# A gated long convolution beside an MLP: a scratch tensor laid out for 128-partition loads, and sums combined by accumulating DMAs

## The chip, the cores and the metric

The kernel runs on one core of a Trainium2 chip. The metric is the device time of one execution in microseconds, the median of several runs. One execution was also recorded by the profiler; its lines are quoted below. In them PE is TensorE (matmuls), PEld its weight loads, DVE is VectorE, ACT is ScalarE, POOL is GpSimd and SP is SyncE, which only issues DMAs here. A "q" behind an engine's name is its instruction queue.

## The reference

Everything is float32. Two branches read the same layer-normalised input, and their results are added to the input. S is 2048, D is 448, F is 1792.

```python
x  = A_q                                    # 1 x 2048 x 448
xn = layernorm(x)                           # over D, eps 1e-5
# branch A: a gated state-space convolution
k_shift = causal depthwise conv of A_k with A_shift_k (4 taps)
kv = k_shift * A_v
y  = irfft(rfft(pad(kv)) * rfft(pad(A_ssm_k)))[:S] + kv * A_ssm_D
A  = xn * y
# branch B: an MLP
h  = xn @ B_w1 + B_b1                       # 448 -> 1792
B  = mish(h) @ B_w2                         # 1792 -> 448
return x + A + B
```

## The kernel before

The 2048 positions are 8 chunks (c0 to c7) of 256 positions, each held as [128 partitions, 2, 448]. The input q and the output have the form [128, 16, 448], so one chunk is 3584 contiguous bytes per partition. The MLP walks the chunks in order. Each chunk has 7 pairs of feature blocks; a pair is worked in two *slots*: an even slot with the first-layer matmuls (`g1_mm`, L447), and an odd slot with the activation on ScalarE (`mish`, L455), its split in a high and a low half (`split`, L74 and L75) and the second-layer matmuls (`g2_mm`, L472 to L474) of the pair two earlier. There are 116 slots. When a chunk's sums are complete, `g2_evac` (L479) adds them to q; for c0 to c5 the result goes to a DRAM scratch tensor ACC, for the last two (`late`: c6, c7) to `out`.

The convolution is worked as a Fourier transform in steps that are put between the MLP's slots by a plan written out by hand: `at(slot, ...)` puts a step ahead of the slot's MLP work, `after(slot, ...)` behind it. Instructions are issued to each engine in this order, and each engine executes its own in order. The forward transforms fill slots up to about 62 and write two scratch tensors (Dh, Dkv). Then come eight octaves (slots 63 to 90): `o_load` reads a part of each (ah, av), `h2_mm`, `v2_mm` transform them (L208), `prod` multiplies them on VectorE, `i1_mm` (L251) does the first step of the inverse, and `i1_out` copies its result to the tile qe (one buffer) and writes it with one DMA from 128 partitions, on ScalarE's queue, to the scratch tensor E (L260).

The last step works on chunks again, two at a time: c6 and c7 at slot 98, c0 and c1 at 102, c2 and c3 at 106, c4 and c5 at 111 (`I2_AT`). For each chunk:

- `e_load` (L284) reads its part of E with two DMAs of 64 partitions each on POOL's queue, into one of four buffers.
- `fold` (L290, L292) forms the sum and the difference of its two halves on VectorE.
- `i2_mm` (L310) does the last transform, 16 small matmuls per chunk; two PSUM buffers.
- `gate` multiplies by the normalised input: two instructions per position row on VectorE, (q - mean) * y at L323 and times rstd plus the MLP's sums at L325. For c6 and c7 the second adds q itself, and the MLP's evacuation later adds the rest.
- `qa_load` (L299, L300) brings q and the sums from ACC for c0 to c5 on SP's queue; each has three buffers, so the loads of c3, c4 and c5 wait until the outputs of c0, c1 and c2 have gone.
- `gate_out` (L330) writes c0 to c5 to `out` on SP's queue.

The layer-norm statistics of the next chunk are small VectorE steps in a list (`drip`); `dv()` takes the next of it between other VectorE work. Their last step has a power on POOL and the normalisation that waits for it. The tiles of the last step share memory with those of the octaves, so a first use waits for the tile that lay there.

Of the kernel before, what the change touches and what calls it, by code (L numbers as in the profile page):

```python
# [7 lines left out]
F32 = mybir.dt.float32  # L8
F32R = mybir.dt.float32r
AF = mybir.ActivationFunctionType  # L10
ALU = mybir.AluOpType
# [16 lines left out]
POOL_H = {20: (0, 2)}  # L28
H0_AT = 63
OCT_AT = (65, 3)  # L30
I2_AT = {98: (6, 7), 102: (0, 1), 106: (2, 3), 111: (4, 5)}
LATE = 2
WARM = 4
WARM_N = 448
# [3 lines left out]
def tile_kernel(ctx: ExitStack, tc, q, k, v, sk, hT, sD, w1, b1, w2, c_f1, c_g, c_gi, c_i2, out):  # L38
# [15 lines left out]

    Dh = dp.tile([NO * 16, 32, D], F32, name="Dh")
    Dkv = dp.tile([NO * 16, 32, D], F32, name="Dkv")
    E = dp.tile([64, NJ * 4, D], F32, name="E")
    ACC = dp.tile([128, NJ, D], F32, name="ACC")

    f1id = cp.tile([128, 2, 128], F32, name="f1id")  # L60
    f1, ident = f1id[:, 0], f1id[:, 1]
# [21 lines left out]
    def dv(n=1):  # L83
        for _ in range(n):
            if drip:
                drip.pop(0)()
# [4 lines left out]
    def at(slot, fn, *args):  # L91
        plan.setdefault(int(slot), []).append((fn, args))
# [163 lines left out]
    def i1_out(o):  # L256
        qe = t2([128, 4, D], "qe")
        for i, p in enumerate(PS.pop(("I", o))):
            nc.scalar.copy(qe[:, 2 * i:2 * i + 2], p[:, :, :D])
        nc.scalar.dma_start(E[8 * o:8 * o + 8].rearrange("(t r) p d -> (r p) t d", t=4), qe)  # L260


    ph3 = ExitStack()
# [3 lines left out]
    def t3(shape, name, bufs=2):  # L267
        if not sp3:
            ph2.close()
            sp3.append(ph3.enter_context(tc.tile_pool(name="ph3", bufs=2, reuse_waits="tile")))  # L270
            i2 = sp3[0].tile([128, 2, 32], F32, name="i2", bufs=1)
            nc.sync.dma_start(i2, c_i2)
            sp3.append(i2)
        return sp3[0].tile(shape, F32, name=name, bufs=bufs)

    def late(c):
        return c >= NCHUNK - LATE

    def e_load(c):

        e = EE[c] = t3([128, 2, 2, D], "e3", 4)
        src = E.rearrange("(h k) (m j b) d -> j k m h b d", h=2, m=2, b=2)
        for jj in range(2):
            nc.gpsimd.dma_start(e[64 * jj:64 * jj + 64].rearrange("p h b d -> p h (b d)"),  # L284
                              src[2 * c + jj].rearrange("k m h b d -> (k m) h (b d)"))

    def fold(c):
        e = EE[c]
        x = t3([128, 2, D], "ex")
        V.tensor_add(x, e[:, 0], e[:, 1])  # L290
        dv()
        V.tensor_sub(e[:, 1], e[:, 0], e[:, 1])  # L292
        dv()
        EE[c] = x, e[:, 1]

    def qa_load(c):
        if not late(c):
            qt, ac = t3([128, 2, D], "q3", 3), t3([128, 2, D], "a3", 3)
            nc.sync.dma_start(qt, q[:, 2 * c:2 * c + 2])  # L299
            nc.sync.dma_start(ac, ACC[:, 2 * c:2 * c + 2])  # L300
            QA[c] = qt, ac

    def i2_mm(c):
        p = pc()
# [8 lines left out]

    def gate(c):
        p = PS.pop(("P", c))
        if late(c):
            x, o, e, f = Q[c], t3([128, 2, D], "z", 1), Q[c], Q[c]
        else:
            qt, ac = QA[c]
            x, o, e, f = qt, qt, ac, qt  # L320
        for jj in range(2):
            j = 2 * c + jj
            V.scalar_tensor_tensor(o[:, jj], x[:, jj], mv[:, j, 0:1], p[:, jj, :D], op0=ALU.subtract, op1=ALU.mult)  # L323
            dv()
            V.scalar_tensor_tensor(f[:, jj], o[:, jj], rstd[:, j:j + 1], e[:, jj], op0=ALU.mult, op1=ALU.add)  # L325
            dv()

    def gate_out(c):
        if not late(c):
            nc.sync.dma_start(out[:, 2 * c:2 * c + 2], QA.pop(c)[0])  # L330


    RW = {}
# [142 lines left out]
    def g2_evac(c, jjs=(0, 1)):  # L476
        x = Q[c]
        for jj in jjs:
            V.tensor_add(x[:, jj], P2.pop((c, jj))[:, :D], x[:, jj])  # L479
            dv()  # L480
            if late(c):
                nc.sync.dma_start(out[:, 2 * c + jj], x[:, jj])
        if not late(c):
            nc.sync.dma_start(ACC[:, 2 * c:2 * c + 2], x)

    def mlp_slot(s):
        i, half = divmod(s, 2)
# [81 lines left out]
    ts = sorted(I2_AT)  # L569
    for n, t in enumerate(ts):  # L570
        for m, c in enumerate(I2_AT[t]):
            at(ts[n - 2] + 1 if n > 1 else ts[0] - 4 + n, e_load, c)
            at(ts[n - 1] + (2 if m else -2 if n == 2 else -1) if n > 1 else ts[0] - 5 + m, qa_load, c)
            after(t - 3, fold, c)
            at(t, i2_mm, c)
            after(t, gate, c)
            at(t + 2 + m, gate_out, c)

    V.memset(rstd, 0.0)
    V.memset(mhalf, -0.5)  # L580
# [53 lines left out]
def _constants():  # L634
# [10 lines left out]
    f1 = np.stack([Wo.real, Wo.imag], axis=4).reshape(64, 128)  # L645
    f1 = np.concatenate([f1, f1])

    i2 = np.stack([W.real.T, W.imag.T], axis=1)[:32].reshape(4, 2, 4, 2, 64).transpose(0, 2, 1, 3, 4).reshape(64, 2, 32) / 2048
    i2 = np.concatenate([i2, i2])
    n2 = np.arange(32)[:, None] // 2 + 16 * (np.arange(32)[:, None] % 2)  # L650
    k2 = np.arange(32)[None, :]
# [2 lines left out]
    for kk in range(64):  # L654
        o, r, t = kk // 8, kk // 4 % 2, kk % 4
        g = w(n2 * (4 * kk - 1) + 256 * n2 * k2)
        G[r, 0, :, o, t, 0], G[r, 1, :, o, t, 0] = g.real, -g.imag
        G[r, 0, :, o, t, 1], G[r, 1, :, o, t, 1] = g.imag, g.real

        gt = g.T.reshape(32, 16, 2)  # L660
        GI[t, :, o, r, 0, 0], GI[t, :, o, r, 1, 0] = gt.real, gt.imag
        GI[t, :, o, r, 0, 1], GI[t, :, o, r, 1, 1] = -gt.imag, gt.real
    c = lambda a: np.ascontiguousarray(a, dtype=np.float32)
    return dict(c_f1=c(np.stack([f1, np.eye(128)], axis=1)), c_g=c(G.reshape(128, 8, 4, 2, 32)), c_gi=c(GI.reshape(128, 8, 2, 2, 64)),
                c_i2=c(i2))
# [27 lines left out]
```

## Time and profile before

| What | us |
|---|---|
| Median of 3 runs (375.63 to 376.65) | 376.12 |
| The profiled execution | 375.92 |
| Its span, first to last instruction | 373.9 |
| PE busy | 362.3 |
| DVE busy | 269.1 |
| ACT busy | 158.7 |
| POOL busy | 67.4 |

The span is what the trace shows; the time of the same execution is 2.0 us more. Busy times are shares of the whole span, and the stages differ, so what matters in a stage is read from its own windows and timelines. A row of a timeline has the start and the duration in us, the engine, the line, the operation, what it writes and reads, and the number of merged instructions; a bracket at its end gives the idle time of the engine before it and what ended that. A matmul's duration includes the pipeline, so that rows overlap.

### The profile page before, as it was taken

How to read it: one execution, taken by the hardware profiler on the slowest of the kernel's cores; microseconds unless marked ns; L12 is line 12 of the kernel's file. 1: busy time of each engine (PE TensorE's matmuls, PEld its weight loads, DVE VectorE, ACT ScalarE, POOL GpSimd, SP SyncE). 2: the span in 40 equal slices, each digit the busy share in tenths (PEclk: the TensorE clock that was granted, in tenths of full speed). 3: DMA queues.
4: the chain of work that ended last, by engine and by line, in shares of the span. 5: the costliest groups of instructions: out<-in, count | busy, mean ns of one | idle time of the engine just before them, and what ended most of it. 6: DMA issues, size and time to landing. Idle time of an engine off the chain costs nothing.

```text
span 373.9 us, 7487 instructions
## 1 busy us (share of the span) xinstructions
PE 362.3 (97%) x3128; PEld 292.6 (78%) x3128; DVE 269.1 (72%) x370; ACT 158.7 (42%) x265; POOL 67.4 (18%) x57
## 2 busy tenths in 40 slices
PE   8999999999998999999999999999999999999993
PEld 2889888888897988988886666666666799688983
DVE  4899748999959987995445745844854915799683
ACT  2785642443433324333434755553755243213220
POOL 2107002622070225320033000140000005220000
PEclk9999999999999999999999999999999999999998
DMA  8999968657695437604794687868480778999466
GB/s 308 315 319 317 396 232 246 200 162 230 163 297 181 100 66 233 196 3 121 238 296 154 214 272 248 269 236 271 160 295 22 260 285 183 221 196 284 152 199 244
DMA packets 32563, 82.11 MB, mean 220 GB/s; under 512 B 2961, under 2 KB 18194, under 8 KB 32530
## 3 DMA queue, kind: packets, MB, share of 16 engines
q1 hardware_dynamic: 22130, 51.69, 41.5%
q10 hardware_dynamic: 9120, 22.61, 20.1%
q0 software_dynamic: 1280, 7.34, 8.5%
q8 instruction: 24, 0.39, 0.4%
q14 instruction: 9, 0.07, 0.0%
HBM read 53.19 MB, written 28.44 MB: 218 GB/s over the span
## 4 chain that ended last, share of the span: by engine, by line
PE 44%; DMA 10%; DVE 9%; issue 3%; ACT 2%; POOL 1%; DVEq 0%; SPq 0%; POOLq 0%
PE pg L447 17%; PE pc L208 7%; PE pg L472 5%; PE pg L474 5%; PE pg L473 5%; DMA out_dram<-q 4%; PE pc L251 3%; DMA a<-ACC 3%; DMA e<-E 2%; PE pc L125 1%; PE pg L407 1%; DMA E<-qe 1%; DVE ex L290 1%; DVE acl L75 1%; DVE q L325 1%
## 5 line engine op out<-in xcount | busy, mean ns | idle before, releaser
L455 ACT ACTIVATE a<-pg,b1t 128x256 f32<-128x256 f32 x112 | 47.1, 473 | 119.2 <-PE pg L447 103.5
L447 PE MATMUL pg<-XH,w1h 128*128 128x256 f32 x448 | 91.1, 285 | 0.7 <-ACT XH L419 0.7
L447 PEld LDWEIGHTS pg<-XH,w1h 128*128 128x128 f32 x448 | 69.7, 188 | 17.4 <-issue 15.0
L472 PE MATMUL pg<-w2h,ach 128*128 128x448 f32 x224 | 83.1, 371 | 0.0
L473 PE MATMUL pg<-w2l,ach 128*128 128x448 f32 x224 | 81.3, 363 | 0.6 <-DVE w2l L75 0.6
L474 PE MATMUL pg<-w2h,acl 128*128 128x448 f32 x224 | 81.4, 363 | 0.0
L75 DVE TENSOR_TENSOR acl<-a,ach 128x512 fp32r<-128x512 f32 x56 | 38.7, 691 | 50.4 <-ACT ach L74 50.3
L447 PE MATMUL pg<-XL,w1h 128*128 128x256 f32 x448 | 69.6, 277 | 0.0
L447 PEld LDWEIGHTS pg<-XL,w1h 128*128 128x128 f32 x448 | 59.4, 188 | 0.1
L447 PE MATMUL pg<-XH,w1l 128*128 128x256 f32 x336 | 56.8, 278 | 0.0
L472 PEld LDWEIGHTS pg<-w2h,ach 128*128 128x128 f32 x224 | 42.0, 187 | 12.3 <-issue 9.4
L447 PEld LDWEIGHTS pg<-XH,w1l 128*128 128x128 f32 x336 | 46.8, 188 | 0.1
L473 PEld LDWEIGHTS pg<-w2l,ach 128*128 128x128 f32 x224 | 42.1, 188 | 3.5 <-DVE w2l L75 1.1
L474 PEld LDWEIGHTS pg<-w2h,acl 128*128 128x128 f32 x224 | 42.1, 188 | 2.6
L388 POOL TENSOR_TENSOR rstd<-ve,mhalf 128x2 f32<-128x2 f32 (+1 forms) x9 | 8.5, 948 | 167.6 <-DVE ve L385 162.4
L74 ACT CAST ach<-a 128x512 fp32r<-128x512 f32 x56 | 34.7, 620 | 1.8
L155 POOL TENSOR_TENSOR x<-kr,skb 128x896 f32<-128x896 f32 x8 | 17.0, 2129 | 74.8 <-DVE x L154 54.1
L172 DVE TENSOR_TENSOR x<-x 128x896 f32<-128x896 f32 x24 | 26.6, 1106 | 5.1 <-POOL x L155 4.4
L392 POOL TENSOR_SCALAR xn<-qt,mv,rstd 128x448 f32<-128x448 f32 x12 | 26.8, 2240 | 0.6
L419 ACT CAST XH<-pg 128x512 fp32r<-128x512 f32 x16 | 9.4, 588 | 37.6 <-PE pg L407 37.4
L131 ACT COPY st<-pc 128x896 f32<-128x896 f32 x16 | 14.5, 908 | 14.8 <-PE pc L125 14.8
L417 DVE TENSOR_TENSOR XL<-pg,XH 128x512 fp32r<-128x512 f32 x16 | 10.9, 687 | 13.5 <-ACT XH L419 13.3
(65 smaller groups left out, 399.9 us busy)
## 6 DMA issues: line engine op xcount, KB each, us to landing
Dh<-st ACTq DMA_DIRECT2D x16, 448.0 KB, 5.9
Dkv<-st ACTq DMA_DIRECT2D x16, 448.0 KB, 5.1
ah<-Dh SPq DMA_DIRECT2D x8, 896.0 KB, 5.4
av<-Dkv SPq DMA_DIRECT2D x8, 896.0 KB, 4.9
E<-qe ACTq DMA_DIRECT2D x8, 896.0 KB, 4.2
e<-E POOLq DMA_DIRECT2D x16, 448.0 KB, 10.3
kr<-in_k_dram SPq DMA_DIRECT2D x10, 448.0 KB, 6.3
kr<-in_w_dram SPq DMA_DIRECT2D x7, 512.0 KB, 5.8
```

The source lines that it names most:

```text
L74: nc.scalar.copy(h, raw)
L75: V.tensor_sub(l, raw, h)
L131: nc.scalar.copy(st[:, 1], o)
L155: nc.gpsimd.tensor_mul(o, KR[g - u // 2], skb[:, u:u + 1].to_broadcast([128, 2, D]))
L172: V.tensor_add(KV[g], KV[g], o)
L208: nc.tensor.matmul(p[32 * t:32 * t + 32, r, :D], g[rs, t, c], a[rs, t], start=True, stop=True, tile_position=(64 * r, 32 * t))
L392: eng.tensor_scalar(xn[:, jj, :D], Q[c][:, jj], mv[:, j, 0:1], rstd[:, j:j + 1], op0=ALU.subtract, op1=ALU.mult)
L447: nc.tensor.matmul(ps[:, n], l, r, start=n_ == 0, stop=n_ == len(mm) - 1)
L455: nc.scalar.activation(a[:, n], ps[:, n], AF.Mish, bias=b1t[:, 2 * p + n:2 * p + n + 1])
L472: nc.tensor.matmul(ps, ah[:, n, cs], w2h[:, f], start=f == 0, stop=False)
L473: nc.tensor.matmul(ps, ah[:, n, cs], w2l[:, f], start=False, stop=False)
L474: nc.tensor.matmul(ps, al[:, n, cs], w2h[:, f], start=False, stop=f == NF - 1)
```

## The change

E is laid out anew: its rows come in another order (the constants of `i1_mm` and `i2_mm` are permuted to match), so that a chunk's part is one load of 128 partitions, and the write of an octave is two DMAs of 64 partitions each. ACC is gone: `g2_evac` writes the MLP's sums of c0 to c5 to `out`, and `gate_out` adds the gated product to them by an accumulating DMA on POOL's queue. The gate of c0 to c5 has one VectorE instruction and a ScalarE multiply by rstd per row. `q_load` loads only q, with five buffers and one of the MLP's; c0 and c1 at slot 92 on SP's queue, c2 to c5 at slot 94 on POOL's. The loads of E for the first two pairs come at slots 92 and 93. The second chunk of a pair is folded and gated one slot behind the first, and the last pair is at slot 110 instead of 111, both gates directly behind it. The statistics list is emptied at slot 91.

```diff
-I2_AT = {98: (6, 7), 102: (0, 1), 106: (2, 3), 111: (4, 5)}
+I2_AT = {98: (6, 7), 102: (0, 1), 106: (2, 3), 110: (4, 5)}
...
-    E = dp.tile([64, NJ * 4, D], F32, name="E")
-    ACC = dp.tile([128, NJ, D], F32, name="ACC")
+    E = dp.tile([NJ * 4, 64, D], F32, name="E")
...
-        nc.scalar.dma_start(E[8 * o:8 * o + 8].rearrange("(t r) p d -> (r p) t d", t=4), qe)
+        for r in range(2):
+            k = 8 * (o % 4) + 4 * r
+            nc.scalar.dma_start(E.rearrange("p (k h) d -> p k h d", h=2)[:, k:k + 4, o // 4], qe[64 * r:64 * r + 64])
...
         e = EE[c] = t3([128, 2, 2, D], "e3", 4)
-        src = E.rearrange("(h k) (m j b) d -> j k m h b d", h=2, m=2, b=2)
-        for jj in range(2):
-            nc.gpsimd.dma_start(e[64 * jj:64 * jj + 64].rearrange("p h b d -> p h (b d)"),
-                              src[2 * c + jj].rearrange("k m h b d -> (k m) h (b d)"))
+        nc.gpsimd.dma_start(e.rearrange("p b h d -> p b (h d)"),
+                            E.rearrange("(b x) (k h) d -> x k b (h d)", b=2, h=2)[4 * c:4 * c + 4].rearrange("x k b d -> (x k) b d"))
...
-        V.tensor_add(x, e[:, 0], e[:, 1])
+        V.tensor_add(x, e[:, :, 0], e[:, :, 1])
         dv()
-        V.tensor_sub(e[:, 1], e[:, 0], e[:, 1])
+        V.tensor_sub(e[:, :, 1], e[:, :, 0], e[:, :, 1])
         dv()
-        EE[c] = x, e[:, 1]
-
-    def qa_load(c):
-        if not late(c):
-            qt, ac = t3([128, 2, D], "q3", 3), t3([128, 2, D], "a3", 3)
-            nc.sync.dma_start(qt, q[:, 2 * c:2 * c + 2])
-            nc.sync.dma_start(ac, ACC[:, 2 * c:2 * c + 2])
-            QA[c] = qt, ac
+        EE[c] = x, e[:, :, 1]
+
+    def q_load(c, eng=nc.sync):
+        QA[c] = mp.tile([128, 2, D], F32, name="qt", tag="qt", bufs=3) if c == 5 else t3([128, 2, D], "q3", 5)
+        eng.dma_start(QA[c], q[:, 2 * c:2 * c + 2])
...
     def gate(c):
         p = PS.pop(("P", c))
-        if late(c):
-            x, o, e, f = Q[c], t3([128, 2, D], "z", 1), Q[c], Q[c]
-        else:
-            qt, ac = QA[c]
-            x, o, e, f = qt, qt, ac, qt
         for jj in range(2):
             j = 2 * c + jj
-            V.scalar_tensor_tensor(o[:, jj], x[:, jj], mv[:, j, 0:1], p[:, jj, :D], op0=ALU.subtract, op1=ALU.mult)
+            r = rstd[:, j:j + 1]
+            x = (Q if late(c) else QA)[c][:, jj]
+            o = t3([128, D], "z") if late(c) else x
+            V.scalar_tensor_tensor(o, x, mv[:, j, 0:1], p[:, jj, :D], op0=ALU.subtract, op1=ALU.mult)
             dv()
-            V.scalar_tensor_tensor(f[:, jj], o[:, jj], rstd[:, j:j + 1], e[:, jj], op0=ALU.mult, op1=ALU.add)
-            dv()
+            if late(c):
+                V.scalar_tensor_tensor(x, o, r, x, op0=ALU.mult, op1=ALU.add)
+                dv()
+            else:
+                nc.scalar.mul(x, x, r)
 
     def gate_out(c):
         if not late(c):
-            nc.sync.dma_start(out[:, 2 * c:2 * c + 2], QA.pop(c)[0])
+            nc.gpsimd.dma_start(out[:, 2 * c:2 * c + 2], QA.pop(c), accum_op=ALU.add)
...
-            nc.sync.dma_start(ACC[:, 2 * c:2 * c + 2], x)
+            nc.sync.dma_start(out[:, 2 * c:2 * c + 2], x)
...
-            at(ts[n - 2] + 1 if n > 1 else ts[0] - 4 + n, e_load, c)
-            at(ts[n - 1] + (2 if m else -2 if n == 2 else -1) if n > 1 else ts[0] - 5 + m, qa_load, c)
-            after(t - 3, fold, c)
+            at(ts[n - 2] + 1 if n > 1 else ts[0] - 6 + n, e_load, c)
             at(t, i2_mm, c)
-            after(t, gate, c)
+            after(t if t == ts[-1] else t + m, gate, c)
             at(t + 2 + m, gate_out, c)
+            after(t - 4 + m if n else t - 3 + m, fold, c)
+    for c in range(NCHUNK - LATE):
+        at(ts[0] - (6 if c < 2 else 4), q_load, c, nc.sync if c < 2 else nc.gpsimd)
+
+    at(ts[0] - 7, lambda: dv(len(drip)))
```

More of the change, by code (lines that the diff above doesn't have):

```diff
@@ L646, in _constants @@
     f1 = np.concatenate([f1, f1])
-    i2 = np.stack([W.real.T, W.imag.T], axis=1)[:32].reshape(4, 2, 4, 2, 64).transpose(0, 2, 1, 3, 4).reshape(64, 2, 32) / 2048
+    i2 = np.stack([W.real.T, W.imag.T])[:, :32].reshape(64, 2, 32) / 2048
     i2 = np.concatenate([i2, i2])
@@ L658, in _constants @@
         G[r, 0, :, o, t, 1], G[r, 1, :, o, t, 1] = g.imag, g.real
-        gt = g.T.reshape(32, 16, 2)
-        GI[t, :, o, r, 0, 0], GI[t, :, o, r, 1, 0] = gt.real, gt.imag
-        GI[t, :, o, r, 0, 1], GI[t, :, o, r, 1, 1] = -gt.imag, gt.real
+        gt = g.T.reshape(32, 16, 2).transpose(0, 2, 1)
+        GI[t, :, o, r, 0, ..., 0], GI[t, :, o, r, 1, ..., 0] = gt.real, gt.imag
+        GI[t, :, o, r, 0, ..., 1], GI[t, :, o, r, 1, ..., 1] = -gt.imag, gt.real
     c = lambda a: np.ascontiguousarray(a, dtype=np.float32)
```

## The prediction

> **What bounds the kernel now.** I read the head of the page first, then the windows of the last stage, the timelines of TensorE and VectorE there, and last the chain of waits.
>
> ```profile
> span 373.9 us, 7487 instructions
> PE 362.3 (97%) x3128; PEld 292.6 (78%) x3128; DVE 269.1 (72%) x370; ACT 158.7 (42%) x265; POOL 67.4 (18%) x57
> PE   8999999999998999999999999999999999999993
> ```
>
> TensorE is busy 97% of the span, so only two things can shorten this kernel: holes in TensorE's row, and what lies behind its last matmul. The change touches the work from some 200 us on, its core lies behind 300. There the windows (columns: time, length, then busy time of PE, PEld, DVE, ACT, POOL, the granted clock, DMA share, GB/s) show one hole of over half a microsecond, at 320 to 324, and the end from 368 on:
>
> ```profile
> 320.00:322.00 2.00, 1.45 (x20) 0.14 (x4) 1.96 (x2) 0.00 (x0) 1.03 (x2) 1.00 1.01 219
> 322.00:324.00 2.00, 1.82 (x21) 0.99 (x20) 2.00 (x4) 0.00 (x0) 0.54 (x2) 1.00 1.02 222
> 368.00:370.00 2.00, 0.23 (x2) 0.00 (x0) 1.97 (x4) 0.00 (x0) 0.00 (x0) 1.00 0.21 84
> ```
>
> TensorE's timeline around the hole. The third column is the duration, the bracket is what ended the idle time:
>
> ```profile
> 319.62 0.57 PE L310 MATMUL pc<-ex,i 64*32 64x448 f32 x2
> ...
> 321.15 0.94 PE L310 MATMUL pc<-ex,i 64*32 64x448 f32 x4 [0.55 <-DVE ex L290]
> ...
> 323.18 0.62 PE L447 MATMUL pg<-XH,w1h 128*128 128x256 f32 x3
> ...
> 333.20 0.57 PE L310 MATMUL pc<-ex,i 64*32 64x448 f32 x2
> ...
> 334.86 0.62 PE L447 MATMUL pg<-XH,w1h 128*128 128x256 f32 x3
> ```
>
> A pair of chunks of the last transform (line 310) takes 334.86 - 333.20 = 1.66 us when nothing is late, but at slot 98 it takes 323.18 - 319.62 = 3.56 us. So 1.90 us is lost there, to the second chunk of the pair (c7). VectorE's timeline says why:
>
> ```profile
> 303.03 0.69 DVE L75 TENSOR_TENSOR acl<-a,ach 128x512 fp32r<-128x512 f32 x1 [4.66 <-ACT ach L74]
> ...
> 315.88 1.09 DVE L290 TENSOR_TENSOR ex<-e 128x896 f32<-128x896 f32 x1 [1.30 <-DMA e<-E]
> ...
> 320.01 1.09 DVE L290 TENSOR_TENSOR ex<-e 128x896 f32<-128x896 f32 x1 [1.91 <-DMA e<-E]
> 321.13 1.09 DVE L292 TENSOR_TENSOR e<-e 128x896 f32<-128x896 f32 x1
> 322.14 0.68 DVE L417 TENSOR_TENSOR XL<-pg,XH 128x512 fp32r<-128x512 f32 x1
> ```
>
> The fold of c6 starts at 315.88 on the landing of its load of E, that of c7 at 320.01 on its own. The split of the next normalised tile (XL, line 417) stands behind that fold. After 323.18 TensorE has no hole up to its last matmul. The end:
>
> ```profile
> 367.87 0.37 PE L474 MATMUL pg<-w2h,acl 128*128 128x448 f32 x1
> ```
> ```profile
> 365.88 0.68 DVE L323 SCALAR_TENSOR_TENSOR q<-q,mv,pc 128x448 f32<-128x448 f32 x1 [1.85 <-DMA q<-in_q_dram]
> 366.97 0.69 DVE L325 SCALAR_TENSOR_TENSOR q<-q,rstd,a 128x448 f32<-128x448 f32 x1 [0.41 <-DMA a<-ACC]
> ...
> 368.88 1.15 DVE L479 TENSOR_TENSOR qt<-pg,qt 128x448 f32<-128x448 f32 x2
> ```
> ```profile
> 369.00 0.33 SPq L330 DMA_DIRECT2D out_dram<-q  x1
> 369.53 0.95 SPq L482 DMA_DIRECT2D out_dram<-qt  x2
> ```
> ```profile
> 356.09 5.32 DMA out_dram<-q
> 361.43 0.33 SPq L299
> ```
>
> The last matmul ends at 368.24, but VectorE starts the two last evacuations only at 368.88 and ends them at 370.03, since the gate of c5 stands before them and waits for q and for the partial sums a. These came late, because their load at 361.43 waits for a buffer that an output (issued 356.09) frees.
>
> **The change, part by part.**
>
> *Loads of E on all partitions.* Sixteen loads of 448 KB to 64 partitions become eight of 896 KB to 128. What their width is worth stands in the windows:
>
> ```profile
> 128.00:129.00 1.00, 1.00 (x12) 1.00 (x11) 0.97 (x2) 0.00 (x0) 0.00 (x0) 1.00 0.98 197
> 129.00:130.00 1.00, 1.00 (x8) 0.95 (x7) 1.00 (x3) 0.70 (x2) 0.00 (x0) 1.00 1.01 297
> 316.00:318.00 2.00, 2.00 (x16) 1.95 (x16) 1.97 (x2) 0.68 (x2) 0.00 (x0) 1.00 1.00 219
> 298.00:302.00 4.00, 4.00 (x42) 3.35 (x27) 0.37 (x2) 2.21 (x4) 0.00 (x0) 1.00 1.02 404
> ```
> ```profile
> 308.69 4.94 POOL L284 DMA_DIRECT2D e<-E  x8 [4.09 <-ACT ach L74]
> ```
> ```profile
> 300.46 4.14 DMA E<-qe
> ...
> 307.67 0.04 POOLq L284
> ```
>
> From 316 to 318 only loads of E run: every DMA engine is busy (1.00) and moves 219 GB/s together. From 298 to 302 the 128-partition loads of q and a run: also busy, 404 GB/s. A chunk (0.917 MB) thus takes 4.1 us now (the folds' starts, 315.88 and 320.01, are 4.13 apart) and should take 2.3. The Trainium skill (SBUF — State Buffer, "Door 1: The DMA port swizzle") says that partitions 0 to 63 reach 8 of 16 ports and gives 196 GB/s at 1 MiB against 328 for all 128; the trace agrees, with 219 against 404.
>
> When does c7 land? POOL's loads start at 308.69, one us after its wait ended at 307.67; that wait is for the last write of E, issued at 300.46 (the chain draws its bar only to 304.60, where POOL's instruction before ended). c6 was usable at 315.88, that is 7.2 us after the first issue, 4.1 of it transfer, so 3.1 is fixed. The write of E becomes the counterpart: one DMA from 128 partitions becomes two from 64, on ScalarE's queue. The windows 128 to 130 hold only such half-width writes: 197 GB/s while one runs, 297 where two overlap. So each write takes up to 0.917 MB / 197 = 4.7 us in place of about 2.3, and 0.37 more for the second issue: 2.8 us dearer. Against that, four of the six 448 KB loads (q and a of c0 to c2) that filled the engines ahead of that write no longer stand there: two of them, q of c0 and c1, remain; 4 x 0.459 MB / 404 = 4.5 us less. I take 307.67 + 2.8 - 4.5 = 306.0 for POOL's wait, with ends 303.2 (no dearer write) and 310.5 (no saving). Then c6 is usable at 306.0 + 1.0 + 3.1 + 2.3 = 312.4, and c7 at 314.7.
>
> The new order on VectorE is fold of c6 (2.1 us, 320.01 to 322.14), XL (0.6), fold of c7 (2.1). It can start where VectorE now begins to wait for c6, at 315.88 - 1.30 = 314.6, and ends at 319.4; c7's matmuls are due half a pair (0.83) after 319.62, at 320.45. So the hole closes: **-1.90 us**. At the bad end (310.5) c7 lands at 319.2, its fold ends at 321.3, and 0.9 of the 1.9 stays.
>
> In the octave stage the same dearer writes meet the loads of the next octave:
>
> ```profile
> ah<-Dh SPq DMA_DIRECT2D x8, 896.0 KB, 5.4
> ```
> ```profile
> 226.87 0.38 SPq L195 DMA_DIRECT2D ah<-Dh  x1
> ```
> ```profile
> 225.04 1.73 PE L208 MATMUL pc<-ah,g 64*32 64x448 f32 x32
> ...
> 237.99 1.73 PE L208 MATMUL pc<-ah,g 64*32 64x448 f32 x32
> ```
>
> A load issued at 226.87 lands 5.4 us later and is needed at 237.99: 5.7 us to spare against 2.8. So nothing is paid there; were that cover gone, it would be up to 2.8 us for each of seven octaves.
>
> *No partial sums to load, q early.* The six loads of a go, and q is loaded for all chunks by slot 94: c0 and c1 on SP, c2 to c5 on POOL's queue behind the first four loads of E. None waits for an output any more, so no gate stands on a DMA at the end. *The gate* of c0 to c5 loses its second VectorE instruction and gets a ScalarE multiply and an accumulating DMA:
>
> ```profile
> L325 DVE SCALAR_TENSOR_TENSOR q<-q,rstd,a 128x448 f32<-128x448 f32 x12 | 8.2, 685 | 1.3 <-DMA a<-ACC 0.9
> ```
> ```profile
> L455 ACT ACTIVATE a<-pg,b1t 128x256 f32<-128x256 f32 x112 | 47.1, 473 | 119.2 <-PE pg L447 103.5 <-DMA Dkv<-st 10.2 <-DMA Dh<-st 3.4
> L131 ACT COPY st<-pc 128x896 f32<-128x896 f32 x16 | 14.5, 908 | 14.8 <-PE pc L125 14.8
> ```
>
> Twelve times 0.685 = 8.2 us leave VectorE; twelve multiplies of 128x448 reach ScalarE at 0.47 (128x256) to 0.91 (128x896), say 0.55: 6.6 us, 10.9 at most. ScalarE sits idle 119 us before its activations, waiting for TensorE, so this costs nothing. The activation queued behind the last multiplies may start 0.2 us late by them, and its tile is needed two second-layer groups later. VectorE has two folds, two gates and two splits to do per pair of chunks, by these rows 4.4 + 2.7 + 1.4 = 8.5 us of the 334.86 - 323.18 = 11.7 that TensorE takes; only behind slot 98, where c6 and c7 keep both instructions, it is 11.2.
>
> *The last pair at slot 110, one slot earlier.* Its 32 matmuls move ahead of the last first-layer group and cost the same 1.66 us. Both last gates are then done some 8 us before the last matmul, which ends at 368.24 - 1.90 = 366.34, and the evacuations follow it at once: the last ends at 366.95 in place of 370.03. Of these 3.08 us, 1.90 are the hole: **-1.18 us**. The ends are 0, if something else stands there, and 2.3: the 448 KB output issued at 369.00 goes ahead of the final ones today, and the 0.459 MB at 404 GB/s that it takes (1.1 us) may be saved too.
>
> *Draining the statistics at slot 91.* VectorE waits some us for POOL's power there; its row at 303.03 shows 4.66 us of idle time that covers it.
>
> *Accumulating DMAs.* Six outputs move from SP's queue to POOL's, where each waits for ScalarE's multiplies. All of POOL's loads stand ahead of the first of them (slots 92 to 103 against 104), so only accumulates queue behind an accumulate. The four loads of q stand between those of c1 and c2: by the same arithmetic c1 lands at 319.3, q at 323.8, c3 by 328.4, and c2's fold comes at some 334, so they are hidden. No run here has an accumulate. Bounds from rows:
>
> ```profile
> DMA to landing us min/median/max: 2.5/5.2/9.6
> ```
> ```profile
> DMA to landing us min/median/max: 5.1/10.3/16.2
> ```
>
> An output of such a size lands 2.5 us after its issue at best, a load on POOL's queue 16.2 at worst. The row nearest is the first load of E, alone on POOL's queue: 3.1 fixed. To this I add twice a full-width transfer (2 x 0.459 MB / 404 = 2.3), since the old sums have to be read as well: 5.4 us. With the hole gone, the gate of c4 is through VectorE and ScalarE at about 357.5 and that of c5 at 359; so the two land at 362.9 and 365.2. The last outputs are now issued at 370.1 (369.53, two in 0.95), land 2.5 later at 372.6, and 1.3 later the span ends; they will be issued at 367.0 and land at 369.5. So the accumulates stay hidden by 4 us. By the Trainium skill (DMA: Bandwidth & Descriptors, "Anatomy of one DMA") a DMA on POOL's path takes about 2.0 us plus bytes / 436 GB/s; an estimate from it is 3.1 us for 448 KB, and the sum would be the same.
>
> **Sum.** The profiled execution took 375.92 (span 373.9 and 2.0 around it); it lies 0.2 below the median of 376.12. 375.92 - 1.90 - 1.18 = 372.84; on the median's footing **373.0**.
>
> **Rivals.**
>
> *Accumulates set the end (slower).* The place is POOL's queue from slot 104, about 336, on; the price is the time t for which one accumulate holds the engines (2.3 in the sum). With c4's issued at 357.5 they end before the last outputs while 357.5 + 3.1 + 2t < 369.5, so t under 4.4 us (104 GB/s). From t = 5.6 us (82 GB/s) on all six, from 336 + 3.1, end after the 372.6 of today: slower than before. At t = 8.3 (a quarter of 219 GB/s) they end near 389, 16 us slower. With the 16.2 us of the worst row c5 lands at 375.2, and the time is 375.2 + 1.3 + 2.0 = 378.5. For it: a read more per byte, and POOL's queue is the one whose rows are long. Against: those rows are long since loads queue there at half width. The Trainium skill (DMA: Bandwidth & Descriptors, "Rules for kernel authors") says that an accumulate reads its destination and writes it later; no run here shows it.
>
> *The hole stays in part.* The half-width writes of E delay the loads; it starts when c7 lands after 317.3 and costs up to 1.9: 373.9 at the bad end, 374.9 with the whole hole back. For it: 197 GB/s. The Trainium skill (SBUF — State Buffer, "Can I just issue two DMAs to hit both halves?") says two half-width DMAs serialize; the trace has 297 where they overlap, so it agrees only in part, and the row decides.
>
> *No gain.* The change doesn't do what it says: a 128-partition load of E is no faster than its halves. c7 then lands at 306.0 + 1.0 + 3.1 + 8.2 = 318.3, just in time, but with the dearer write (310.5) at 322.8: a hole of 4.5 in place of 1.9 eats the gain of the end, 375.5 to 377.5. Against it: 404 GB/s.
>
> *VectorE or ScalarE late elsewhere (slower).* Behind slot 98 VectorE has 0.5 us to spare in 11.7, and a multiply that waits for VectorE holds the activation behind it on ScalarE. If TensorE misses its tile by 2 us in each of three pairs, that is 6 - 3.1 more: 379.
>
> **How the numbers follow.** A measurement of this kernel tells apart some 0.3%, 1.1 us: faster is under 375.0, slower over 377.2. Both gains: 0.64 (own range 371.9 to 373.9). Hole in part: 0.12, of it 0.10 faster and 0.02 same. Accumulates at the end: 0.14, of it 0.04 faster, 0.02 same, 0.08 slower. No gain: 0.06, same. Late elsewhere: 0.04, slower. So faster 0.78, same 0.10, slower 0.12. The range goes from 371.9, the sum with 2.3 saved at the end, to 376.4, which takes in the partial cases and half of the no-gain case, and leaves out the slower ones.
>
> **What the profile would show.** Right: line 310's 32 matmuls at slot 98 in 1.7 us with no idle bracket; eight loads of E at over 350 GB/s; no wait for q or a; the last evacuation within 0.1 us of its matmul; accumulates landing under 10 us after their issue. Wrong: windows after 340 with a full DMA share at low GB/s and a landing of POOL's output as the last event, or idle TensorE <- ScalarE or VectorE between 325 and 366.

## The result and the profile after

| Kernel | Median (us) | Runs | Range of the runs | Ratio of times to before, 95% interval |
|---|---|---|---|---|
| before | 376.73 | 6 | 375.63 to 381.61 | |
| changed | 372.23 | 6 | 371.46 to 373.1 | 0.9885 [0.9855, 0.9915] |

The kernel became 1.15% faster; predicted were 373.0 us, in a range of 371.9 to 376.4. The ratios leave out slow runs, those over 1.5% above the fastest of their kernel; here that is the one of 381.61. The profiled execution of the changed kernel took 372.4 us, its span 370.5, against 375.92 and 373.9 before. The head of its page:

```profile
span 370.5 us, 7467 instructions
PE 361.2 (98%) x3128; PEld 292.2 (79%) x3128; DVE 261.4 (71%) x358; ACT 165.9 (45%) x277; POOL 71.2 (19%) x59
```

TensorE's busy time hardly changed (361.2 against 362.3), the span is 3.46 us shorter. Windows of the last stage (time, length, busy time of PE, PEld, DVE, ACT, POOL, granted clock, DMA share, GB/s):

```profile
316.00:318.00 2.00, 2.00 (x17) 1.96 (x16) 2.00 (x3) 0.46 (x2) 0.00 (x0) 1.00 1.02 409
320.00:322.00 2.00, 2.00 (x36) 0.82 (x23) 1.29 (x3) 0.00 (x0) 0.77 (x2) 1.00 1.01 405
322.00:324.00 2.00, 2.00 (x20) 2.00 (x19) 1.97 (x4) 0.00 (x0) 0.67 (x1) 1.00 1.03 410
342.00:344.00 2.00, 2.00 (x24) 1.20 (x30) 0.69 (x1) 0.42 (x1) 0.00 (x0) 1.00 1.08 185
```

TensorE is now busy all through 320 to 324, where it had 1.45 and 1.82 of 2.00. The DMA engines, just as full as before (1.01 to 1.03), move 405 to 410 GB/s in place of some 220. From 316 to 318 these are loads of E on 128 partitions, from 320 on mostly those of q behind them, which are as wide. At 342 accumulates run: full engines, 185 GB/s. TensorE's timeline around slot 98 and at the end:

```profile
319.83 0.57 PE L307 MATMUL pc<-ex,i 64*32 64x448 f32 x2
...
321.03 0.54 PE L307 MATMUL pc<-e,i 64*32 64x448 f32 x2
321.50 0.62 PE L446 MATMUL pg<-XH,w1h 128*128 128x256 f32 x3
...
366.20 0.37 PE L473 MATMUL pg<-w2h,acl 128*128 128x448 f32 x1
```

The pair takes 321.50 - 319.83 = 1.67 us, and no row has an idle bracket: the hole of 1.90 is gone. VectorE's timeline:

```profile
314.71 1.08 DVE L289 TENSOR_TENSOR ex<-e 128x896 f32<-128x896 f32 x1
...
316.84 0.68 DVE L416 TENSOR_TENSOR XL<-pg,XH 128x512 fp32r<-128x512 f32 x1
317.44 1.08 DVE L289 TENSOR_TENSOR ex<-e 128x896 f32<-128x896 f32 x1
...
366.61 0.62 DVE L478 TENSOR_TENSOR qt<-pg,qt 128x448 f32<-128x448 f32 x1 [0.58 <-PE pg L473]
```

Neither fold waits for a load now: that of c6 follows other work, that of c7 follows the split of XL, in the order that the change gives. The last evacuation starts 0.04 after its matmul's end (366.57) and waits for that alone. What the DMA queues do in the last 16 us (sums per queue, then the issues with the us from issue to landing; q0 is POOL's queue):

```profile
q0 software_dynamic: 387, 1.22, 46.7%
out_dram<-q POOLq DMA_DIRECT2D x1, 448.0 KB, 5.2
out_dram<-qt POOLq DMA_DIRECT2D x1, 448.0 KB, 7.4
out_dram<-qt SPq DMA_DIRECT2D x2, 224.0 KB, 1.9
```
```profile
308.21 3.18 POOL L283 DMA_DIRECT2D e<-E  x4 [8.62 <-ACT ach L73]
...
358.28 0.86 POOL L329 DMA_DIRECT2D out_dram<-q  x1 [5.30 <-ACT q L324]
359.48 0.86 POOL L329 DMA_DIRECT2D out_dram<-qt  x1 [0.34 <-ACT qt L324]
```

The two last accumulates are issued at 358.28 and 359.48 and land at 363.4 and 366.9; the last output, issued at 367.26, lands at 369.2, and 1.3 later the span ends. Put together, from the end of the last matmul to the end of the span it was 373.94 - 368.24 = 5.70 us and is 370.48 - 366.57 = 3.91.

### The profile page after: what moved, and what is told of

Its sections match the earlier page's. It is cut to its first block, busy times and chain, and to the rows that moved or that the text cites. A ratio compares the mean times of both kernels' runs of the same rounds, so it can differ in the third digit from the quotient of the medians.

```text
span 370.5 us, 7467 instructions
## 1 busy us (share of the span) xinstructions
PE 361.2 (98%) x3128; PEld 292.2 (79%) x3128; DVE 261.4 (71%) x358; ACT 165.9 (45%) x277; POOL 71.2 (19%) x59
## 3 DMA queue, kind: packets, MB, share of 16 engines
q0 software_dynamic: 2336, 11.93, 11.3%
## 4 chain that ended last, share of the span: by engine, by line
PE 62%; DVE 4%; ACT 2%; ACTq 1%; issue 1%; DVEq 0%
PE pg L446 24%; PE pg L471 8%; PE pg L473 8%; PE pg L472 8%; PE pc L207 7%; PE pc L250 3%; PE pc L307 2%; PE pc L124 1%; PE pg L406 1%; ACTq L261 1%; ACT a L454 1%; DVE x L171 1%; DVE yc L240 1%; DVE qt L478 0%; ACT XH L418 0%
## 5 line engine op out<-in xcount | busy, mean ns | idle before, releaser
L471 PEld LDWEIGHTS pg<-w2h,ach 128*128 128x128 f32 x224 | 42.0, 187 | 11.6 <-issue 9.4
L416 DVE TENSOR_TENSOR XL<-pg,XH 128x512 fp32r<-128x512 f32 x16 | 10.9, 687 | 15.5 <-ACT XH L418 15.3
```

The costliest lines, as they stand in the source:

```text
L471: nc.tensor.matmul(ps, ah[:, n, cs], w2h[:, f], start=f == 0, stop=False)
```

## The experiments

Whole times of one kernel scatter by up to 1.3% (371.82 to 376.67 for the changed kernel run again), in part for reasons that lie ahead of anything changed here (the last section has one), so besides them I compare stages of the traces. In the table, *lead* is the time from POOL's first load of E to the start of slot 98's matmuls, *hole* what the pair at slot 98 takes above 1.66, *lag* from the end of the last matmul to the end of the last evacuation, and *rest* from the start of slot 98 to the end of the span. All in us.

| Kernel | Median (runs) | Ratio to before, 95% | Lead | Hole | Lag | Rest |
|---|---|---|---|---|---|---|
| before | | | 10.9 | 1.90 | 1.80 | 54.32 |
| changed | 372.23 (6) | 0.9885 [0.9855, 0.9915] | 11.6 | 0 | 0.66 | 50.65 |
| changed, again | 373.15 (6) | 0.9913 [0.9858, 0.9967] | 11.0 | 0 | 0.66 | 50.65 |
| layout_only | 373.26 (10) | 0.9918 [0.9886, 0.9949] | 7.7 | 1.39 | 0.66 | 52.10 |
| sums_only | 373.93 (10) | 0.9938 [0.9905, 0.9971] | 11.7 | 1.46 | 0.66 | 52.28 |
| layout_moved | 375.86 (10) | 0.9996 [0.9959, 1.0034] | 9.6 | 2.43 | 0.66 | 53.05 |
| layout_behind | 371.79 (4) | 0.987 [0.9778, 0.9962] | 11.4 | 0 | 0.66 | 50.47 |
| plain_out | 372.49 (4) | 0.9897 [0.9861, 0.9933] | 11.1 | 0 | 0.66 | 50.64 |
| pair111 | 373.23 (1) | | 11.6 | 0 | 0.66 | 52.17 |
| pair112 | 378.42 (1) | | 11.1 | 0 | 0.66 | 53.50 |
| q_late | 374.04 (1) | | 10.1 | 0 | 0.66 | 50.37 |
| fold_both | 371.06 (1) | | 11.3 | 0 | 0.66 | 50.65 |
| two_queues | 373.03 (10) | 0.9885 [0.9848, 0.9922] | 12.1 | 0 | 0.66 | 50.63 |
| pool_half | 371.78 (4) | 0.9895 [0.9845, 0.9946] | 11.1 | 0 | 0.66 | 50.64 |

The rest carries the verdicts: it is the same to 0.02 us in both traces of the changed kernel.

### One part alone: the layout (layout_only)

The kernel before with E's new layout, its half-width writes and 128-partition loads, and nothing else of the change:

```diff
-    E = dp.tile([64, NJ * 4, D], F32, name="E")
+    E = dp.tile([NJ * 4, 64, D], F32, name="E")
...
+        for r in range(2):
+            k = 8 * (o % 4) + 4 * r
+            nc.scalar.dma_start(E.rearrange("p (k h) d -> p k h d", h=2)[:, k:k + 4, o // 4], qe[64 * r:64 * r + 64])
...
+        nc.gpsimd.dma_start(e.rearrange("p b h d -> p b (h d)"), ...)
```

> The kernel before with only the new layout of E: one load of 128 partitions per chunk and two half-width writes per octave. Slots, folds, ACC, q and a loads and gates stay as before. Theory W (the width of the loads closes the hole at slot 98): POOL's first load comes at about 309 to 310, the fold of c7 starts by 317.5 instead of 320.0, line 310 takes under 2.0 us at slot 98 instead of 3.56, the end keeps its 1.8 us between the last matmul and the last evacuation, and the time is 374.2 to 374.9. Theory Q (what closes the hole is that fewer loads stand ahead of the last write of E): with six loads still ahead and a dearer write, POOL's first load comes at 310 to 311.5, 0.9 or more of the hole stays, and the time is 375.2 or more.

Its chain of waits (start, duration, what), then VectorE and TensorE around slot 98:

```profile
300.90 9.60 DMA E<-qe
...
312.53 6.56 DMA e<-E
```
```profile
316.86 1.09 DVE L290 TENSOR_TENSOR ex<-e 128x896 f32<-128x896 f32 x1 [2.66 <-DMA e<-E]
...
319.11 1.09 DVE L290 TENSOR_TENSOR ex<-e 128x896 f32<-128x896 f32 x1
```
```profile
321.38 0.57 PE L310 MATMUL pc<-e,i 64*32 64x448 f32 x2 [0.18 <-DVE e L292]
```

The last write of E, issued at 300.3 and 300.9, holds POOL until 310.5, since five of the six loads of q and a were issued on SP just ahead of it, from 295.7 to 298.7, and share the engines with it. So the loads of E start at 311.58, 7.7 us ahead of slot 98 in place of 10.9. Once started they are as fast as they should be: c6 is usable 5.3 us after the first issue and c7 7.5 us after it (319.09), against 7.2 and 11.3 before. Of the hole 1.39 us remain. So width alone is not enough, as Theory Q had it. Neither theory had the end: it came right by itself (lag 0.66), without any change to the gate, and so the time is 373.26 and not the 375.2 or more of Theory Q. The loads for c5 leave 38.6 us after the start of slot 98 instead of 41.8, and c5's gate, the one that held the last evacuations, is done before the last matmul. A likely reason is that the outputs and the loads of q and a no longer queue beside slow loads of E; which of them gained the 3.2 us was not taken apart.

### The other part alone: the sums (sums_only)

The changed kernel with E, its write, its loads and its constants as before; the accumulates, early q, the order and slot 110 remain:

```diff
-            nc.scalar.dma_start(E.rearrange("p (k h) d -> p k h d", h=2)[:, k:k + 4, o // 4], qe[64 * r:64 * r + 64])
+        nc.scalar.dma_start(E[8 * o:8 * o + 8].rearrange("(t r) p d -> (r p) t d", t=4), qe)
...
+        for jj in range(2):
+            nc.gpsimd.dma_start(e[64 * jj:64 * jj + 64].rearrange("p h b d -> p h (b d)"), ...)
```

> The changed kernel with the old layout of E: two loads of 64 partitions per chunk, one write of 128 partitions per octave. Everything else is as changed. Theory W: loads at 219 GB/s bring c7's fold to 318.6 or later, a hole of 0.3 to 1.7 us stays at slot 98, and the time is 372.6 to 374.0. Theory Q: with two loads instead of six ahead of the write, POOL's first load comes at 306 to 307.5, c7's fold starts by 318, the hole is under 0.2, and the time is 372.2 or a little less, since the hole that the longer issue opened near 270 goes too.

```profile
314.80 1.09 DVE L289 TENSOR_TENSOR ex<-e 128x896 f32<-128x896 f32 x1 [0.80 <-DMA e<-E]
...
318.99 1.09 DVE L289 TENSOR_TENSOR ex<-e 128x896 f32<-128x896 f32 x1 [1.37 <-DMA e<-E]
```
```profile
307.38 5.00 POOL L283 DMA_DIRECT2D e<-E  x8 [8.58 <-ACT a L454]
```

POOL starts early (lead 11.7), but the loads take their old time: c6 is folded 7.4 us after the first issue and c7 11.6 after it. The hole keeps 1.46 us, as Theory W had it. Taken together the two runs size the condition. In layout_only the fold of c7 was late by 1.39 at the point where TensorE waited, so the fold has to start by 319.11 - 1.39 = 317.7, 1.5 us ahead of slot 98 (319.24); sums_only gives the same 1.5. Loads of full width need a lead of 7.5 + 1.5 = 9.0 us, halves 11.6 + 1.5 = 13.1. layout_only needs 9.0 and has 7.7; sums_only has 11.7 and needs 13.1. Only both parts together pass, with 11.6 against 9.0.

### Moving the loads of q and a (layout_moved, layout_behind)

If that is so, layout_only needs no accumulating DMA, only its six loads out of the way. The first attempt put them four slots later on SP's queue:

```diff
-            at(ts[n - 1] + (2 if m else -2 if n == 2 else -1) if n > 1 else ts[0] - 5 + m, qa_load, c)
+            at(ts[n - 1] + (2 if m else -2 if n == 2 else -1) if n > 1 else ts[0] - 1 + m, qa_load, c)
```

> The kernel layout_only with one more edit: the loads of q and a of c0 and c1 move from slots 93 and 94 to 97 and 98, behind the last write of E. ACC, the gates with two VectorE instructions and the plain outputs stay; nothing accumulates. Theory J (the hole closes when the loads of E are both wide and early, whatever makes them so): POOL's first load comes by 308.5 counted as in the changed kernel (16.5 us or less ahead of... the start of slot 98 it is 10.5 to 12 us), line 310 takes 1.7 us at slot 98, the end has 0.7 us from the last matmul to the last evacuation as in layout_only, and the time equals the changed kernel's, 372.2 within 0.3%. Theory K (the accumulating DMAs and the shorter gates are needed): VectorE or a late q leaves at least 0.7 us, 373 or more, also against the changed kernel's runs on the same chip.

```profile
299.86 0.42 SPq L299 DMA_DIRECT2D q<-in_q_dram  x1
...
310.35 0.72 SPq L300 DMA_DIRECT2D a<-ACC  x1
```
```profile
318.77 1.09 DVE L290 TENSOR_TENSOR ex<-e 128x896 f32<-128x896 f32 x1 [3.70 <-DMA e<-E]
...
321.03 1.09 DVE L290 TENSOR_TENSOR ex<-e 128x896 f32<-128x896 f32 x1
```

The edit did not do what it was for. SP has nothing to do in those slots, and its queue isn't tied to them: it issues a load as soon as the memory that the load takes is free; the one at 309.51 waited 9.1 us for the landing of the last write of E. Three loads still went out ahead of the write of E (the last at 299.86), the other three at 309.51 to 310.35, right ahead of POOL's first load at 310.54. c6 was usable only 8.2 us after that, not 5.3, and the hole grew to 2.43. It tests neither theory as meant, but shows that traffic beside the loads of E delays c6 and c7 as traffic ahead of the write does.

The second attempt put the same six loads (c0 to c2) on POOL's queue behind the first four loads of E, so that they can't pass them:

```diff
-    def qa_load(c):
+    def qa_load(c, eng=nc.sync):
...
-            at(ts[n - 1] + (2 if m else -2 if n == 2 else -1) if n > 1 else ts[0] - 5 + m, qa_load, c)
+            at(ts[n - 1] + (2 if m else -1) if n > 1 and c > 2 else ts[0] - 2, qa_load, c, nc.gpsimd if c < 3 else nc.sync)
```

> The kernel layout_only with the loads of q and a of c0, c1 and c2 on POOL's queue behind the first four loads of E (slot 96), where they can stand neither ahead of the last write of E nor beside the loads of c6 and c7. ACC, the two-instruction gates and the plain outputs stay; nothing accumulates, nothing runs on ScalarE. Theory J (the hole closes once no other load holds the engines between the last write of E and the landing of c7; accumulates and shorter gates play no part): the load of c6 is usable 6.0 to 6.5 us after POOL's first issue, that issue comes 10.5 us or more ahead of slot 98, line 310 takes at most 1.9 us there, the last evacuation ends 0.7 us after the last matmul, and from slot 98's start to the span's end it is 50.6 to 51.0 us as in the changed kernel. Theory K (accumulates and shorter gates are needed): 1 us or more of the hole stays, or TensorE waits for VectorE or a gate for a later on, and it is 51.6 or more.

```profile
307.97 3.13 POOL L284 DMA_DIRECT2D e<-E  x4 [1.46 <-ACT ach L74]
311.09 0.57 POOL L299 DMA_DIRECT2D q<-in_q_dram  x1
```
```profile
314.29 1.08 DVE L290 TENSOR_TENSOR ex<-e 128x896 f32<-128x896 f32 x1
...
316.42 1.08 DVE L290 TENSOR_TENSOR ex<-e 128x896 f32<-128x896 f32 x1
```

The hole is gone (lead 11.4, both folds without a wait), the lag is 0.66 and the rest 50.47, 0.18 less than in the changed kernel. So the whole gain comes from two things: loads of full width, and fewer loads ahead of the last write of E. This kernel keeps ACC, loads the partial sums and has the long gate. The accumulates, the ScalarE multiplies, the new order on VectorE and slot 110 are not needed for the gain; in this change they are the means by which the loads disappear.

### What the accumulates cost (plain_out, pair111, pair112)

plain_out writes the gated product over the output instead of adding it:

```diff
-            nc.gpsimd.dma_start(out[:, 2 * c:2 * c + 2], QA.pop(c), accum_op=ALU.add)
+            nc.gpsimd.dma_start(out[:, 2 * c:2 * c + 2], QA.pop(c))
```

> The changed kernel with the six accumulating DMAs as plain writes on the same queue; it leaves out the MLP's sums of c0 to c5, which are overwritten. If the accumulates are hidden, as predicted: 372.2, within 0.3%, with the last plain write landing some 2 to 3 us earlier than the 366.9 of the accumulate and the last output at the same place. If the accumulates cost time (their engine time is on the path of the last outputs): 0.5 to 1.5 us faster. The packets show the price: 128 of 3584 B in 140 ns each instead of 291.

The DMA queues of plain_out in the same last 16 us:

```profile
q0 software_dynamic: 160, 0.92, 14.1%
out_dram<-q POOLq DMA_DIRECT2D x1, 448.0 KB, 2.8
out_dram<-qt POOLq DMA_DIRECT2D x1, 448.0 KB, 2.9
```

Two plain writes (0.92 MB) fill 14.1% of 16 us, 1.13 us each. The accumulates need 46.7% for 1.22 MB, that is 7.47 us, or 2.8 us for each 0.459 MB: two and a half times as much. The last plain write lands at 362.6, 4.3 us ahead of the accumulate's 366.9, where 2 to 3 had been expected. The rest stays at 50.64, so in the changed kernel all of it is hidden.

How far is it hidden? pair111 and pair112 put the last pair one and two slots later:

```diff
-I2_AT = {98: (6, 7), 102: (0, 1), 106: (2, 3), 110: (4, 5)}
+I2_AT = {98: (6, 7), 102: (0, 1), 106: (2, 3), 111: (4, 5)}
```

> The changed kernel with the last pair back at slot 111. Theory A (the accumulates are hidden, with 2.3 us between the landing of the last one and of the last output): the pair comes 2.6 us later, the last accumulate lands at about 369.5, near the last output's 369.2, and the time is 0 to 0.4 us over the changed kernel's. Theory B (they have the 4 us of room that was predicted): no difference, and the last accumulate lands before 367.5.

> The changed kernel with the last pair at slot 112, 5.0 us later than at 110. Theory A: the last accumulate lands at about 371.9, 2.7 us behind the last output, and sets the end: 374.9 to 375.3. Theory B: 1 us behind it at most, 373.4 or less. If accumulates never set the end: 372.4.

The queues in the last 14 us of pair111, then of pair112:

```profile
out_dram<-qt POOLq DMA_DIRECT2D x1, 448.0 KB, 6.5
out_dram<-qt SPq DMA_DIRECT2D x2, 224.0 KB, 3.8
```
```profile
out_dram<-qt POOLq DMA_DIRECT2D x1, 448.0 KB, 7.1
out_dram<-qt SPq DMA_DIRECT2D x2, 224.0 KB, 5.2
```

In pair111 the last accumulate is issued at 362.38 and lands at 368.9, before the last output (issued 366.52, landed 370.0). Reckoned by landings alone, as in Theory A, it costs nothing or 0.4 at most. It costs 1.52: the outputs land 3.8 us after their issue (median of the two) instead of 1.9, since they share the engines with the end of the accumulate. In pair112 it is issued at 367.46 and lands at 374.6, and it still isn't the last to land: the last output is issued at 370.33 and lands at 375.1, 4.8 us later instead of 1.9. The rest grows by 2.85. That is near the 2.7 of Theory A, but by luck: the accumulate doesn't set the end by its own landing, it delays the outputs, as in pair111. layout_behind has the last pair at slot 111 too, with plain outputs, and its rest is 50.47; so it is the accumulates that cost, not the slot. Slot 110 is the last of the three at which they are free. pair112's whole time, 378.42, has some 3 us more in it that were lost at its start (last section).

### Early q, and the order on VectorE (q_late, fold_both)

```diff
-        QA[c] = mp.tile([128, 2, D], F32, name="qt", tag="qt", bufs=3) if c == 5 else t3([128, 2, D], "q3", 5)
+        QA[c] = t3([128, 2, D], "q3", 3)
...
-        at(ts[0] - (6 if c < 2 else 4), q_load, c, nc.sync if c < 2 else nc.gpsimd)
+        at({0: 92, 1: 92, 2: 100, 3: 104, 4: 105, 5: 108}[c], q_load, c)
```

> The changed kernel with the loads of q as late as before: three buffers, SP's queue, slots 92, 92, 100, 104, 105, 108, so that c3, c4 and c5 wait until the accumulates of c0, c1 and c2 have landed. Theory E (early loads of q freed the end): c5's q waits for a landing at about 352 or later, its gate is late, and the last evacuation or the last accumulate comes 0.5 us or more later: 372.9 or more. Theory S (the outputs leave soon enough, since no gate waits for a; five buffers weren't needed): q of c5 lands by 356, the gate of c5 starts as now near 357.2, no difference.

```profile
361.18 1.27 DVE L318 SCALAR_TENSOR_TENSOR q<-q,mv,pc 128x448 f32<-128x448 f32 x2 [1.84 <-DMA q<-in_q_dram]
```

With three buffers c5's q waits for an accumulate to free one, and its gate starts after 1.84 us of idle time, 3.1 after that of c4 and not 1.2. The rest is 50.37, no longer than with the early load. So the early load isn't what gains. The whole time, 374.04, would speak for Theory E, but this execution was already 1.7 us behind the changed kernel's at the first octave.

```diff
-            after(t - 4 + m if n else t - 3 + m, fold, c)
+            after(t - 4 + m if n else t - 3, fold, c)
```

> The changed kernel with both folds of the first pair behind slot 95, as before, so that the split XL stands behind the fold of c7. Since c7 lands at about 316 now, the fold of c7 ends by 319 and XL by 319.7, ahead of its use at 321.6: no hole and no difference. If the order had closed part of the hole: line 307 takes over 1.8 us at slot 98, or line 446 behind it waits for XL.

The folds of c6 and c7 back to back, ahead of the split of XL: hole 0, rest 50.65. With a lead of this size the order doesn't matter either.

### The half-width writes (two_queues, pool_half)

The prediction put 0.37 us on the second issue of the write of E, on ScalarE, and nothing on the path. The trace of the changed kernel has a small new wait in the octaves. ScalarE, then TensorE, then the writes of E as a group (duration in ns: least, median, most), line 261 of the changed kernel and line 260 of the one before:

```profile
265.48 2.91 ACTq L261 DMA_DIRECT2D E<-qe  x2
268.43 0.58 ACT L418 CAST XH<-pg 128x512 fp32r<-128x512 f32 x1 [2.98 <-issue]
```
```profile
269.88 1.79 PE L207 MATMUL pc<-av,g 64*32 64x448 f32 x32 [0.30 <-ACT hs L218]
```
```profile
L261 ACTq DMA_DIRECT2D E<-qe x16: 581/612/2297, 211.0 to 301.3; - x16
```
```profile
L260 ACTq DMA_DIRECT2D E<-qe x8: 366/366/397, 211.2 to 300.5; - x8
```

A half-width issue takes 0.61 us against 0.37, and one of the sixteen took 2.30. ScalarE stood 2.98 us behind these two, its next copy came late and TensorE waited 0.30 for it. In the second trace of the changed kernel (the section after this one) two issues took that long, and more came on top: one half landed only 10.4 us after its issue. There is one buffer qe, so the next copy into it waited 2.86 us for that landing, and TensorE then waited 0.62 for ScalarE:

```profile
267.41 10.36 DMA E<-qe
```
```profile
277.87 1.72 ACT L258 COPY qe<-pc 128x896 f32<-128x896 f32 x2 [2.86 <-DMA E<-qe]
```
```profile
284.95 1.79 PE L207 MATMUL pc<-av,g 64*32 64x448 f32 x32 [0.62 <-ACT hs L218]
```

Two kernels move one of the two halves to another queue, SP's or POOL's; both also leave the last octave's `dv()` in `prod` out:

```diff
-            nc.scalar.dma_start(E.rearrange("p (k h) d -> p k h d", h=2)[:, k:k + 4, o // 4], qe[64 * r:64 * r + 64])
+            (nc.scalar, nc.gpsimd)[r].dma_start(E.rearrange("p (k h) d -> p k h d", h=2)[:, k:k + 4, o // 4], qe[64 * r:64 * r + 64])
```

> The changed kernel with two edits: the second half of each write of E goes to SP's queue, and the products of the last octave take no statistics between them. If the 1.25 us (once 2.9) that ScalarE spends on issuing two half-width writes opened the 0.30 us hole ahead of line 207 near 270, and the statistics the one of 0.41 at slot 90, TensorE's row loses both: 371.5 in place of 372.2. Rival: the half on SP's queue waits for ScalarE's copy and holds the next octave's loads behind it; then TensorE waits for ah or av, and the time is 372.5 or more.

> The changed kernel with the second half of each write of E on POOL's queue, and no statistics between the products of the last octave. ScalarE then issues one half-width write, 0.6 us instead of 1.25 to 2.9 us: the hole of 0.30 ahead of line 207 and the one of 0.41 at slot 90 go, from the first matmul on ah to the span's end 186.0, and the time is 371.6 to 371.9. Rival: POOL issues late behind its normalisations, the qe buffer comes free late or the last half lands late, and the hole at slot 98 returns: 372.5 or more.

What TensorE waits for (in total, times, longest), changed kernel, then pool_half:

```profile
PE pc L207 <- ACT hs L218: 0.8, 2, 0.5
...
PE pc L250 <- DVE yc L240: 0.4, 1, 0.4
```
```profile
PE pc L207 <- ACT hs L218: 0.5, 1, 0.5
```

Two short waits of 0.3 and 0.4 are gone in pool_half; the second was there before, too. From the first octave's matmul to slot 98 it takes 135.05 us, the changed kernel 136.04 and 136.93 in its two traces, before 135.77. In time that is not to be told from the changed kernel: 371.78 against 372.23, and the intervals of the ratios overlap. two_queues takes 135.52 there. Of it 0.65 is a wait for a load of Dkv (av) at 194.14, ahead of the first write of E, so that its edit isn't the cause; no wait that its rival named shows in the trace. In neither kernel does an issue of a half take over 1 us. The `dv()` and the second queue were not taken apart.

### The changed kernel again

> The changed kernel itself, on the same chip as the other two of this call: 372.2 within 0.3%. From the first matmul on ah to the span's end some 186.7 us, and from slot 98 on 50.65, as in its first trace; what differs between executions lies ahead of that matmul.

373.15 us, and 0.9913 [0.9858, 0.9967]: within the first interval. From slot 98 on it is 50.65 as expected. But from the first matmul on ah to the end it is 187.6, not 186.7: the octaves take 0.89 more than in the first trace, most of it by the late write shown above (TensorE's wait of 0.62). So executions of this kernel differ within the octaves too, not only ahead of them. No version here is faster than the changed kernel by more than the intervals; layout_behind and pool_half are level with it. The two together were not run.

## Why the prediction was right, point by point

**The hole, -1.90: as predicted.** Its steps: c7 was to land 1.0 + 3.1 + 2 x 2.3 = 8.7 us after POOL's wait ends; in layout_only, where the fold does wait for it, it is 319.09 - 310.50 = 8.6. The dearer write was put at 2.8 us; from before to layout_only the lead falls from 10.93 to 7.66, by 3.3. The loads taken away were put at 4.5; from layout_only to the changed kernel the lead grows to 11.62, by 4.0. Both errors go the same way, so POOL's first load came at 308.21, not 307.0. The margin bore it, with a lead of 11.6 where 9.0 are needed. The landing of c7 from which the hole opens was given as 317.3; the prediction's own terms, 320.45 less a fold of 2.1, give 318.35, and by the runs the fold must start 1.5 us ahead of slot 98, at 318.1 on that clock. The rival in which the hole stays in part needs a delay of 2.6 us more; layout_only is that case. Of the Trainium skill (SBUF — State Buffer, "Door 1: The DMA port swizzle") the case bears out that a load on half of the partitions is slower: 404 to 410 GB/s here against 219.

**The end, -1.18: the mechanism right, the size short.** The last evacuation comes 0.66 us after the last matmul in place of 1.80, 1.14 of the 1.18. What the sum left out, and the upper end of the bound had, is the landing: in 1.9 us after the issue in place of 2.6 (before, 370.06 to 372.66), since c5's output of 448 KB no longer stands ahead. That is another 0.66, so the end gave 1.80. But the cause named for it was too narrow: layout_only and sums_only have the same lag with the old gate or the old loads, so either part alone removes this wait.

**The octaves, 0: mis-sized.** The second issue on ScalarE is not quite hidden: 1.25 us for the pair against 0.37 for one write, with one issue of 2.30. From the first octave's matmul to slot 98 the first trace is 0.27 longer than before, the second 1.16. The longer transfer was set against the loads of the next octave alone, which bear it. It also meets the one buffer qe, which the prediction left out: in the first trace ScalarE doesn't wait for it, in the second it waits 2.86 us. The whole by stages, in the first trace: -0.06 ahead of the octaves, +0.27, -1.90, +0.03 from slot 98 to the last matmul and -1.80 behind it are the span's -3.46.

**The accumulates: hidden, with half the margin.** Each holds the engines for 2.8 us (2.3 was taken), lands 5.2 us after its issue when alone (5.4) and 7.4 when another is under way. The last one lands 2.3 us ahead of the last output, where 4 were predicted. The bound at which they end last, 4.4 us, was not reached, but it was the wrong bound: pair111 and pair112 show them costing 1.5 and 2.85 us while they still land ahead of the last output, by delaying the outputs. The Trainium skill (DMA: Bandwidth & Descriptors, "Rules for kernel authors") says that an accumulate reads its destination before it writes; plain_out agrees with 1.13 us against 2.8.

**VectorE and ScalarE: no cost, as predicted.** The twelve multiplies take 0.67 us each (0.55 was taken), and TensorE has no wait behind slot 98. **No gain from the width**: out, by 405 GB/s.

## What to carry to other kernels

A load that comes late has two remedies, to make it faster and to start it sooner, and each may fall short alone: write down the lead that the load needs and the lead that it has, for each part of a change by itself. Look at what stands ahead of the transfer that releases it; here six loads that nobody needed yet cost as much as the slower write. A transfer is hidden only while nothing that shares the DMA engines with it is on the path: it costs before it is the last to land.

## What the runs showed of the hardware

- An accumulating DMA from 128 partitions moved 163 GB/s of its own bytes with full engines (1.22 MB in 7.47 us), a plain one 407 (0.92 MB in 2.26 us), and its issue took POOL 0.86 us against 0.54.
- A write of half the partitions was not a cheaper issue but a dearer one: 0.61 us against 0.37 for the full one on the same queue. In each of the ten traces in which ScalarE issues both halves, one or two of the sixteen issues took 2.0 to 2.4 us; in two_queues and pool_half, where it issues one of them, none did. The two kinds of write also go to DRAM in different patterns, so that the width is what makes the issue dearer isn't shown.
- A short wait at the start may cost more than itself. All kernels here issue the same instructions up to the octaves, and in some executions TensorE waits near 9 us for a load of its input. In pair112 it waits for 1.9 us there, and then the granted clock (the column behind the five busy times) is halved:

```profile
10.00:11.00 1.00, 1.00 (x7) 1.00 (x7) 0.50 (x2) 0.36 (x1) 0.00 (x0) 0.65 1.00 402
14.00:15.00 1.00, 1.00 (x6) 1.00 (x6) 0.97 (x2) 0.35 (x1) 0.00 (x0) 0.50 0.03 11
17.00:18.00 1.00, 1.00 (x9) 1.00 (x9) 0.53 (x1) 0.78 (x2) 0.00 (x0) 0.93 1.02 408
```

The clock is 0.50 from about 10.3 to 17.1. two_queues waited for 2.0 us and has the same; q_late and the second trace of the changed kernel waited for 1.6 and 1.8, and there the clock is 1.00 at this place. 1.8 and 1.9 are too near to each other to call that a threshold, and that the wait is the cause is not shown. The second trace of the changed kernel reached the octaves 1.1 us behind the first, pair112 3.3 us behind it: with nearly the same wait, the other 2.2 go with the halved clock. So whole times of single runs say little here. Why the load comes late in some executions stays open.
